# Second unit's attention values computed from high and low parts, and the low part of g moved to GpSimd in the first MLP, in a fused attention and MLP kernel

## The chip, the cores and the metric

The kernel runs on one core of one Trainium2 chip. The time is that of one execution on the device, in microseconds (us). A core has a matrix engine (TensorE, called PE in the profile, with its weight loads shown apart as PEld), a vector engine (DVE), an activation engine (ACT), a general engine (GpSimd, called POOL), and a queue that issues DMAs (SyncE, called SP). Each engine takes its instructions in a fixed order. PE writes to PSUM; the other tiles named here lie in SBUF unless said otherwise.

## What is computed

Sliding-window attention with four sink keys for 4 batches of 8 heads (768 tokens, head size 64), then an MLP on the result (3072 tokens, 512 to 2048 to 512), all in float32:

```python
scores = scale * np.matmul(q, k.transpose(0, 1, 3, 2))
is_sink = pos[None, :] < int(n_sink)                  # n_sink = 4
in_window = (rel >= 0) & (rel < int(window))          # window = 128
scores = np.where(is_sink | in_window, scores, -1000000000.0)
a = np.exp(scores - np.max(scores, axis=-1, keepdims=True))
a = a / (np.sum(a, axis=-1, keepdims=True) + 1e-09)
x = np.matmul(a, v)        # then [batch*token, 512]
h = x @ w_in
g = np.maximum(0.01 * h, h)
return g @ w_out
```

## The kernel before

**Units.** The work is cut into 8 units of 384 tokens (T = 3 tiles of 128), two to a batch. Each unit has an attention part (8 heads, in 4 pairs) and an MLP part (16 blocks fc of 128 hidden columns). While PE computes the MLP of unit u, it computes the attention of unit u+1 in between; a generator for each gives the next few matmuls, and a due time in the last loop of `fast_path` weaves the two together. PE's order is exactly the order in which the code is written; the orders of DVE, ACT, POOL and SP come from a scheduler that puts instructions in the order of a simulated timeline. Unit 0's attention runs alone at the start (with warm-up matmuls in it); from 61 us on the MLP of unit 0 runs with the attention of unit 1.

**Exact products.** A float32 matmul on the tiles as they are ("native") is issued as two matmuls, each with its own weight load. The other way is to split a tile in a high part (the value rounded to the type fp32r) and a low part (the value minus the high part, rounded again) and to add products of parts, each one fp32r matmul. The MLP does that everywhere: `xh`, `xl` (line 507), `gh`, `gl` (lines 572, 573), and weights `wih`, `wil`, `woh`, `wol`.

**Attention.** For each head and tile j: `scores` (line 314), the softmax on DVE and ACT (lines 334 to 344; result in `pk`), then `tail`, which transposes `pk` on PE and copies it to `pt`. For each pair, `sinks` transposes the four sink columns, and DVE spreads them to `sn` (line 416). Then `values` (line 448) multiplies `pt` and the sinks by the values. In units 0 and 1 (`NATP = 8` pairs) this is done natively: `vn` is the loaded tile itself, 64 columns to a head, and both heads add into one PSUM bank, from which `emit_x` makes `xh` (ACT) and `xl` (DVE). From unit 2 on `split_values` (line 278) makes high and low parts of the loaded `vraw` and `vsraw` side by side in `vsp` and `ssp` (ACT and POOL), `tail` makes a low part of `pt` on DVE, the sinks get one too (`st`, line 423), and a head is 6 or 8 fp32r matmuls with 128 columns of weights and one for the sinks. The two 64-row halves of the result are then added (ACT line 458, DVE line 459) to `xf`.

**Weights.** `w_in` and `w_out` come as 64-bit words. `load_weights` (line 167) loads a 512 KB block into one of two buffers `wraw` (one block of `w_in`, then one of `w_out`, by turns), decodes it on DVE in three instructions (lines 176, 178, 180), and splits it on ACT (line 184) and POOL (line 185). The decode of block fc is issued when the MLP of unit 0 comes to block fc-2; blocks 0 to 2 are decoded in unit 0's attention, so 13 pairs of blocks (3 to 15) are decoded during unit 0's MLP. Both the MLP's g step and the weights' decode stand in DVE's one queue with the softmax.

**Loads of q, k and values.** SP's queue issues them with the weights' loads. A native head pair's values are loaded when the earlier pair has freed its tile (`vfree`), from inside the odd head before (line 489). The q and k of a head (`qkraw`) are split into `qksp` on ACT and POOL one head ahead, just after the first tile's softmax (`split_next`, line 494).

Of the kernel before, what the change touches and what calls it, by code (L numbers as in the profile page):

```python
# [9 lines left out]
F32 = mybir.dt.float32  # L10
F32R = mybir.dt.float32r
# [3 lines left out]
ALU = mybir.AluOpType  # L15
# [13 lines left out]
NU = 2 * B  # L29
NATP = 8  # L30
NATP0 = 0
# [14 lines left out]
LEAD0 = 5  # L46
GLP = 0
NACT = 6
# [73 lines left out]
def fast_path(ctx, tc, cpool, wz, qk, vu, vs, w_in, w_out, out, ident, lim, masks, tri, diag,  # L122
# [154 lines left out]

    def split_values(u, h):
        vr, sr = vraws.pop((u, h))
        vsp = apool.tile([P, 4, 2 * P], F32R, tag="vsp", name=f"vsp{u}_{h}", bufs=1)  # L280
        ssp = phase["late"].tile([SKR, 1, 2 * P], F32R, tag="ssp", name=f"ssp{u}_{h}", bufs=1)
        for dst, src, m in ((vsp, vr, NVB[u % 2]), (ssp, sr, 1)):
            sview = src[:, 0:m * P].rearrange("p (n q c) -> p n q c", q=2, c=D)
            hview = dst.rearrange("p n (q c) -> p n q c", c=D)[:, 0:m, 0::3, :]
            nc.scalar.copy(out=hview, in_=sview)
            nc.gpsimd.tensor_tensor(out=dst[:, 0:m, D:3 * D].rearrange("p n (q c) -> p n q c", c=D),
                                    in0=sview, in1=hview.bitcast(F32), op=ALU.subtract)
        return vsp, ssp
# [74 lines left out]
    def tail_wide(u, h, j, pk, pt, sk):  # L363
        half = u % 2
        tp = slot()
        n = 0
        o = 2 * P * j if half else max(0, (2 * j - 1) * P)
        for at in ((0, WM) if j or half else (0,)):
            nc.tensor.transpose(out=tp[:, n:n + P], in_=pk[:, j, at:at + P], identity=ident)  # L369
            n += P  # L370
        keep_warm(u, WARMT)
        nc.scalar.copy(out=pt[:, 0, o:o + n], in_=tp[:, 0:n])
        if j == T - 1:
            nj = T - 1 + half
            nc.scalar.copy(out=sk[:, 0:nj, h % 2], in_=pk[:, T - nj:, P:WM])
# [30 lines left out]

    def sinks(u, pair, sk):
        half = u % 2
# [10 lines left out]
        if native_values(u, 2 * pair):  # L419
            return sv  # L420
        st = sts[half]
        nc.scalar.copy(out=st[0:rows, :], in_=sv)
# [4 lines left out]
    def values(u, h, pt, st, state):  # L427
# [3 lines left out]
        hp = slice(odd * D, (odd + 1) * D)  # L431
        lp = slice((1 - odd) * D, (2 - odd) * D)
        vv, sv = state["v"]
        if native_values(u, h):
# [29 lines left out]
    def attend(u, h, pend, state):  # L464
# [8 lines left out]
        if not odd:  # L473
            state = state[h // 2 % 2]
            state["v"] = vraws.pop((u, h)) if native_values(u, h) else split_values(u, h)
            state["sk"] = apool.tile([P, T, 2, NSK], F32, tag="sk", name=f"sk{u}_{h // 2}")
        else:
            state = state[h // 2 % 2]
# [8 lines left out]
        for j in range(T):  # L487
            nxt = following(u, h)
            if j and odd and nxt and native_values(*nxt) and nxt not in vraws and (vfree[nxt[1] // 2 % 2] or j > 1):
                load_values(*nxt)  # L490
            ps = scores(u, h, j, parts, rows, sp)
            softmax(u, h, j, ps, pk[:, j, 0:KSL[u % 2][j][1]] if u < WIDE else pk[:, j, :])
            if u < WIDE and j == 0:
                split_next(u, h)
            yield
            at = len(pend) - (VSW and j == 0 and not odd and len(pend) > 0)
            pend.insert(at, lambda j=j: tail(u, h, j, pk, pt, sk))
        if odd:
            def gather():
                state["st"] = sinks(u, h // 2, sk)  # L500
                if u == 0 and h < H - 1:
                    load_weights(h // 2)
# [17 lines left out]
    def attention_stream():  # L520
# [5 lines left out]
        pump()  # L526
        load_values(0, 2)
        for u in range(NU):
# [298 lines left out]
```

## Time and profile before

| | us |
|---|---|
| three runs | 745.74, 746.28 (median), 749.74 |
| the profiled execution | 745.78, with a span of 743.8 in the trace and 1.98 around it |
| PE busy, of the span | 719.4 (97%) |
| DVE busy | 562.5 (76%) |
| ACT busy | 434.0 (58%) |
| POOL busy | 381.4 (51%) |

The span is the time from the first to the last instruction that the trace holds. PE's share of 97% is an average: in the first 61 us, where the attention of unit 0 runs alone, and from there to 158 us, PE has gaps; from there to the last tiles it has almost none. A stretch must be read by itself: how busy each engine is in it, and on which engine a wait ends last. DVE instructions overlap a little at their ends, so that the busy time of a stretch is less than the sum of the durations in it.

### The profile page before, as it was taken

The page shows a single profiled execution, that of the slowest core. Times are in us where ns is not written, and L with a number is a line of the kernel's source. Part 1 is how long each engine was busy: PE and PEld are TensorE (multiplying, and loading weights), DVE is VectorE, ACT ScalarE, POOL GpSimd, SP SyncE. Part 2 cuts the span into 40 slices and gives each one's busy share as a digit, 9 for nine tenths or more (in the row PEclk, how much of TensorE's full clock was granted, in tenths as well). Part 3 has the DMA queues.
Part 4 walks back from the last instruction along what each step waited for, and adds up shares of the span by engine and source line. Part 5 has one row for each costly group of instructions (what it writes and reads, how often), then busy time and mean ns, then how long its engine had stood idle before and what let it go on. Part 6 is the DMA issues. An engine that isn't in the chain of part 4 may idle for free.

```text
span 743.8 us, 12686 instructions
## 1 busy us (share of the span) xinstructions
PE 719.4 (97%) x3935; PEld 624.2 (84%) x3935; DVE 562.5 (76%) x1832; ACT 434.0 (58%) x1208; POOL 381.4 (51%) x490
## 2 busy tenths in 40 slices
PE   8889999989999999999999999999999999999996
PEld 4557777768999988999988988989889899989995
DVE  6866889877667888888888888889888978733222
ACT  4666667657665666666566666666666656532221
POOL 3554455455445677665666587665666555300000
PEclk9979999999999999999999999999999999999999
DMA  5543666543212343224333443334331321001001
GB/s 181 181 146 117 186 196 195 187 146 100 59 51 68 115 125 119 89 93 156 115 108 102 126 137 99 105 96 146 116 110 52 111 69 44 1 1 42 1 1 46
DMA packets 30474, 76.94 MB, mean 103 GB/s; under 512 B 3584, under 2 KB 9152, under 8 KB 30400
## 3 DMA queue, kind: packets, MB, share of 16 engines
q1 hardware_dynamic: 30256, 75.94, 32.7%
q8 instruction: 33, 0.54, 0.3%
q14 instruction: 41, 0.34, 0.1%
q10 hardware_dynamic: 144, 0.13, 0.1%
HBM read 69.76 MB, written 6.29 MB: 102 GB/s over the span
## 4 chain that ended last, share of the span: by engine, by line
PE 84%; DVE 9%; ACT 3%; issue 1%; DMA 1%; POOL 0%; SPq 0%; ACTq 0%; DVEq 0%
PE o L584 32%; PE h L563 32%; PE v L448 9%; PE s L314 5%; PE t L382 2%; PE warm L304 2%; DVE gl L573 2%; PE t L369 1%; DVE zeroi L197 1%; DVE pk L344 1%; ACT qksp L271 1%; DVE g L571 1%; DMA woraw<-in_w_out 1%; DMA qkraw<-in_qk 0%; DVE pk L334 0%
## 5 line engine op out<-in xcount | busy, mean ns | idle before, releaser
L563 PE MATMUL h<-xh,wih 128*128 128x384 f32 x512 | 187.8, 367 | 1.5 <-DVE g L571 1.3
L563 PE MATMUL h<-xh,wil 128*128 128x384 f32 x512 | 173.0, 338 | 1.5 <-POOL wil L185 1.5
L563 PE MATMUL h<-xl,wih 128*128 128x384 f32 x512 | 172.5, 337 | 0.0
L584 PE MATMUL o<-woh,gh 128*128 128x512 f32 x384 | 154.3, 402 | 0.0
L584 PE MATMUL o<-woh,gl 128*128 128x512 f32 x384 | 151.2, 394 | 0.0
L584 PE MATMUL o<-wol,gh 128*128 128x512 f32 x384 | 151.1, 393 | 0.0
L353 POOL TENSOR_SCALAR_AFFINE_SELECT pt<-stg 128x256 fp32r<-128x256 f32 x240 | 101.4, 448 | 83.3 <-DVE stg L395 70.9
L272 POOL TENSOR_TENSOR qksp<-qkraw,qksp 64x524 fp32r<-64x524 f32 (+1 forms) x62 | 75.0, 1209 | 107.2 <-issue 62.7
L573 DVE TENSOR_TENSOR gl<-g,gh 128x384 fp32r<-128x384 f32 x128 | 105.8, 826 | 17.1 <-ACT gh L572 15.6
L571 DVE TENSOR_TENSOR g<-h,g 128x384 f32<-128x384 f32 x128 | 71.1, 555 | 60.2 <-ACT g L570 58.1
L563 PEld LDWEIGHTS h<-xh,wih 128*128 128x128 f32 x512 | 96.6, 189 | 16.1 <-issue 2.9
L570 ACT ACTIVATE g<-h 128x384 f32<-128x384 f32 x128 | 62.2, 486 | 69.7 <-PE h L563 68.4
L338 ACT ACTIVATE pk<-pk,negm 128x128 f32<-128x128 f32 (+2 forms) x168 | 70.2, 418 | 54.0 <-DVE negm L334 53.0
L563 PEld LDWEIGHTS h<-xl,wih 128*128 128x128 f32 x512 | 97.0, 189 | 3.0
L563 PEld LDWEIGHTS h<-xh,wil 128*128 128x128 f32 x512 | 96.2, 188 | 1.8 <-POOL wil L185 1.8
L314 PEld LDWEIGHTS s<-qksp 128*128 128x128 f32 x372 | 68.8, 192 | 21.9 <-issue 10.4
L584 PEld LDWEIGHTS o<-woh,gl 128*128 128x128 f32 x384 | 72.1, 188 | 16.3 <-DVE gl L573 0.2
L572 ACT CAST gh<-g 128x384 fp32r<-128x384 f32 x128 | 65.7, 513 | 33.6 <-DVE g L571 31.3
L314 PE MATMUL s<-qksp 128*128 128x260 f32 (+1 forms) x372 | 77.0, 289 | 8.6 <-DVE pk L344 5.2
L584 PEld LDWEIGHTS o<-woh,gh 128*128 128x128 f32 x384 | 72.5, 189 | 11.2 <-issue 2.4
L584 PEld LDWEIGHTS o<-wol,gh 128*128 128x128 f32 x384 | 72.4, 188 | 6.4
L274 POOL TENSOR_TENSOR qksp<-qkraw,qksp 128x384 fp32r<-128x384 f32 x62 | 67.9, 1095 | 4.7
(124 smaller groups left out, 1222.8 us busy)
## 6 DMA issues: line engine op xcount, KB each, us to landing
qkraw<-in_qk SPq DMA_DIRECT2D x32, 454.0 KB, 4.1
qkraw<-in_qk SPq DMA_DIRECT2D x30, 388.0 KB, 3.3
wiraw<-in_w_in SPq DMA_DIRECT2D x16, 512.0 KB, 3.6
woraw<-in_w_out SPq DMA_DIRECT2D x16, 512.0 KB, 4.0
ciraw<-in_w_in SPq DMA_DIRECT2D x16, 512.0 KB, 3.6
coraw<-in_w_out SPq DMA_DIRECT2D x16, 512.0 KB, 3.8
out<-ob SPq DMA_DIRECT2D x23, 256.0 KB, 2.0
vraw<-in_vu SPq DMA_DIRECT2D x12, 256.0 KB, 2.6
```

The costliest lines, as they stand in the source:

```text
L272: nc.gpsimd.tensor_tensor(out=sp[D:P, TU:TU + n], in0=raw[D:P, TU:TU + n], in1=sp[D:P, TU:TU + n].bitcast(F32), op=ALU.subtract)
L274: nc.gpsimd.tensor_tensor(out=sp[:, TU + n:2 * TU + n], in0=raw[:, 0:TU], in1=sp[:, 0:TU].bitcast(F32), op=ALU.subtract)
L314: nc.tensor.matmul(ps[:, 0:kn], lhsT=sp[rows, off + j * P:off + (j + 1) * P], rhs=sp[rows, TU + k0:TU + k0 + kn], start=c == 0, stop=c == ...
L338: nc.scalar.activation(out=e, in_=e, func=AF.Exp, scale=-1.0, bias=neg, accum_out=sm)
L353: nc.gpsimd.affine_select(out=out, in_=src, pattern=([[0, x]] if x > 1 else []) + [[sign, P]], base=-1 if prev else 0, channel_multiplier= ...
L448: nc.tensor.matmul(out[:, o:o + m], lhsT=l, rhs=r, start=c == 0, stop=c == len(mms) - 1, skip_group_check=True)
L563: nc.tensor.matmul(ph[:, 0:TU], lhsT=w[:, cs], rhs=x, start=cc == 0 and c == 0, stop=cc == NCC - 1 and c == 2)
L570: nc.scalar.mul(g, ph[:, 0:TU], 0.01)
L571: anchor[0] = nc.vector.tensor_tensor(out=g, in0=ph[:, 0:TU], in1=g, op=ALU.max)
L572: nc.scalar.copy(out=gh, in_=g)
L573: (nc.gpsimd if u == 0 and fc % 4 < GLP else nc.vector).tensor_tensor(out=gl, in0=g, in1=gh.bitcast(F32), op=ALU.subtract)
L584: nc.tensor.matmul(po[t], lhsT=gg[:, tsl], rhs=w, start=f == 0 and c == 0, stop=f == NFC - 1 and c == 2)
```

## The change

Native values stay for unit 0 only (`NATP = 4`). Unit 1's values go the way of the later units: high and low parts of the values (ACT, POOL), a low part of `pt` on DVE, and the sum of two halves to `xf`. As the tiles of the later units (`ssp`, `st0`, `st1`) don't exist yet in unit 1, a tile `it` in the place of a buffer that is free after unit 0 takes the sinks (first 384 columns, zeroed by a DVE memset and an ACT copy) and the sinks' values (last 256). Since unit 1 isn't native any more, `emit_x` makes its `xl` on POOL instead of DVE. `GLP = 4` moves the low part `gl` in all 16 blocks of unit 0's MLP from DVE to POOL. Native values (unit 0) are loaded at tile 1 of their own even head. The split of q and k for heads of unit 1 and later in the first two units is issued one tile later.

```diff
-NATP = 8
+NATP = 4
...
-GLP = 0
+GLP = 4
...
+    def interim(u, h):
+        it = phase["early"].tile([SKR, TU + 2 * P], F32R, tag="qkraw2", name=f"it{u}_{h}", bufs=1)
+        zeros = xpool.tile([P, TU], F32, tag="xf", name=f"zeros{u}_{h}")
+        nc.vector.memset(zeros, 0.0)
+        nc.scalar.copy(out=it[:, 0:TU], in_=zeros)
+        return it
+
-    def split_values(u, h):
+    def split_values(u, h, it):
         vr, sr = vraws.pop((u, h))
         vsp = apool.tile([P, 4, 2 * P], F32R, tag="vsp", name=f"vsp{u}_{h}", bufs=1)
-        ssp = phase["late"].tile([SKR, 1, 2 * P], F32R, tag="ssp", name=f"ssp{u}_{h}", bufs=1)
+        if u < WIDE:
+            ssp = it[:, TU:].rearrange("p (o c) -> p o c", o=1)
+        else:
+            ssp = phase["late"].tile([SKR, 1, 2 * P], F32R, tag="ssp", name=f"ssp{u}_{h}", bufs=1)
...
         nc.scalar.copy(out=pt[:, 0, o:o + n], in_=tp[:, 0:n])
+        if not native_values(u, h):
+            nc.vector.tensor_tensor(out=pt[:, 1, o:o + n], in0=tp[:, 0:n], in1=pt[:, 0, o:o + n].bitcast(F32),
+                                    op=ALU.subtract)
...
-        st = sts[half]
+        st = it[:, 0:TU] if u < WIDE else sts[half]
...
+        if native_values(u, h) and not odd:
+            state["v"] = vraws.pop((u, h))
...
-            state["v"] = vraws.pop((u, h)) if native_values(u, h) else split_values(u, h)
+            if not native_values(u, h):
+                state["it"] = interim(u, h) if u < WIDE else None
+                state["v"] = split_values(u, h, state["it"])
...
         for j in range(T):
-            nxt = following(u, h)
-            if j and odd and nxt and native_values(*nxt) and nxt not in vraws and (vfree[nxt[1] // 2 % 2] or j > 1):
-                load_values(*nxt)
+            if j == 1 and not odd and native_values(u, h) and (u, h) not in vraws:
+                load_values(u, h)
             ps = scores(u, h, j, parts, rows, sp)
...
-            if u < WIDE and j == 0:
+            nxt = following(u, h)
+            if u < WIDE and j == min(nxt[0], 1):
                 split_next(u, h)
...
         load_values(0, 0)
         pump()
-        load_values(0, 2)
```

Three places show how the order moves. First, PE, unit 1, head 4 (`v1_4`; `o0_0` is an output tile of unit 0's MLP). Before:

```order
L448 MATMUL v1_4_1642<-pt1_4_1204,vn1_4_1123 64x128
L448 MATMUL v1_4_1642<-pt1_4_1204,vn1_4_1123 64x256 x2
L448 MATMUL v1_4_1642<-pt1_4_1204,vn1_4_1123 64x128
L448 MATMUL v1_4_1642<-sn1_2_1615,vsn1_4_1124 64x384
L584 MATMUL o0_0_888<-woh9_1346,gh0_9_1554 128x512
L584 MATMUL o0_0_888<-wol9_1347,gh0_9_1554 128x512
```

and after the change:

```order
L463 MATMUL v1_4_1732<-pt1_4_1257,vsp1_4_1250 128x128 x2
L463 MATMUL v1_4_1732<-pt1_4_1257,vsp1_4_1250 128x256 x4
L463 MATMUL v1_4_1732<-pt1_4_1257,vsp1_4_1250 128x128 x2
L463 MATMUL v1_4_1732<-it1_4_1246 128x384
L600 MATMUL o0_0_901<-woh9_1404,gh0_9_1634 128x512
L600 MATMUL o0_0_901<-wol9_1405,gh0_9_1634 128x512
```

Five native matmuls (each issued as two) become nine in fp32r; all that stands around a head on PE stays where it was.

Second, DVE, at the end of unit 1 (`wid15` and `wod15` are the decode of the last weights, `pk2_0` with `s2_0_0` and `s2_0_1` the first softmaxes of unit 2, `tri` a mask). Before:

```order
L176 TENSOR_SCALAR wod14_1778<-woraw14_1766 128x512
L178 SCALAR_TENSOR_TENSOR wod14_1778<-woraw14_1766,wod14_1778 128x512
L511 TENSOR_TENSOR xl1_3_1897<-v1_6_1879,xh1_3_1896 128x384
L180 SCALAR_TENSOR_TENSOR wo14_1777<-woraw14_1766,wod14_1778 128x512
L334 ISA pk2_0_1924,negm_65<-s2_0_0_1926,m0_86 128x128
L334 ISA negm_65 128x1
L176 TENSOR_SCALAR wid15_1838<-wiraw15_1833 128x512
L323 COPY_PREDICATED s2_0_1_1937<-tri_88,s2_0_1_1937 128x128
```

and after the change:

```order
L180 SCALAR_TENSOR_TENSOR wi15_1947<-wiraw15_1943,wid15_1948 128x512
L176 TENSOR_SCALAR wod15_1957<-woraw15_1945 128x512
L178 SCALAR_TENSOR_TENSOR wod15_1957<-woraw15_1945,wod15_1957 128x512
L474 TENSOR_TENSOR xf1_3_2001<-v1_7_2010,xf1_3_2001 64x384
L180 SCALAR_TENSOR_TENSOR wo15_1956<-woraw15_1945,wod15_1957 128x512
L344 ISA pk2_0_2050,negm_65<-s2_0_0_2052,m0_86 128x128
L344 ISA negm_65 128x1
L145 MEMSET zeros_2037 128x384
L148 CAST st0_2039<-zeros_2037 128x256
L148 CAST st1_2041<-zeros_2037 128x384
L333 COPY_PREDICATED s2_0_1_2063<-tri_88,s2_0_1_2063 128x128
```

The whole decode of weights 15 now stands ahead of unit 2's first softmax, where before it stood among the first four.

Third, SP, around the load of the q and k of unit 1's head 1 (`qkraw1_1`). Before:

```order
L159 DMA woraw2_533<-in_w_out 128x1024
L239 DMA vn1_0_682<-in_vu1 128x512
L223 DMA qkraw1_1_654<-in_qk1 128x908
L159 DMA wiraw3_678<-in_w_in 128x1024
L240 DMA vsn1_0_683<-in_vs 24x128
L159 DMA woraw3_680<-in_w_out 128x1024
```

and after the change:

```order
L159 DMA woraw2_533<-in_w_out 128x1024
L223 DMA qkraw1_1_672<-in_qk1 128x908
L244 DMA vraw1_0_639<-in_vu1 128x512
L246 DMA vsraw1_0_641<-in_vs 128x128
L159 DMA wiraw3_682<-in_w_in 128x1024
L159 DMA woraw3_684<-in_w_out 128x1024
```

The load of q and k no longer stands behind the load of the values, which waits for a tile that unit 0's third pair frees.

## Rows read from the trace of the kernel before

**Rows 1.** Busy time of each engine in four stretches (start and end, length, then busy us and instructions of PE, PEld, DVE, ACT and POOL, the granted PE clock, the share of the DMA engines, GB/s).

```profile
65.10:159.50 94.40, 89.63 (x464) 70.10 (x465) 80.97 (x206) 64.22 (x164) 51.04 (x43) 1.00 0.59 185
88.00:132.00 44.00, 42.54 (x224) 33.67 (x223) 40.33 (x102) 32.02 (x82) 25.07 (x21) 1.00 0.61 191
135.00:145.00 10.00, 9.37 (x55) 8.09 (x53) 9.66 (x25) 8.12 (x22) 6.84 (x7) 1.00 0.63 201
158.20:656.00 497.80, 496.06 (x2821) 448.43 (x2822) 412.08 (x1394) 311.76 (x890) 303.00 (x415) 1.00 0.31 96
```

**Rows 2.** The chain of waits from 149 to 159 us (start, length, what).

```profile
149.32 2.24 PE v L448 x10
151.59 0.49 ACT xh L510
...
152.57 0.64 DVE wo L180
...
153.28 3.75 DMA woraw<-in_w_out
...
158.22 0.41 PE s L314 x2
```

**Rows 3.** PE in order of time around a native head of unit 1 (start, length, engine, line, operation, tiles, shape; the rows of several matmuls are merged).

```profile
124.72 0.34 PE L563 MATMUL h<-xh,wil 128*128 128x384 f32 x1
124.99 1.51 PE L448 MATMUL v<-pt,vn 128*64 128x128 f32 x8
...
127.56 0.40 PE L584 MATMUL o<-wol,gh 128*128 128x512 f32 x1
```

**Rows 4.** The same around a split head of unit 3, which has the same four key blocks.

```profile
256.51 0.39 PE L584 MATMUL o<-woh,gl 128*128 128x512 f32 x1
256.74 1.02 PE L448 MATMUL v<-pt,vsp 128*128 128x128 f32 x8
...
258.05 0.39 PE L584 MATMUL o<-wol,gh 128*128 128x512 f32 x1
```

**Rows 5.** Transition from unit 0 to unit 1, in order of time: POOL's last read of `qkraw1_0`, SP's issue of `vn1_0` and of `qkraw1_1`, and ACT's split of the latter (in brackets the idle time before, and what ended it); then the first weight decode of the next stretch.

```profile
43.87 1.01 POOL L274 TENSOR_TENSOR qksp<-qkraw,qksp 128x384 fp32r<-128x384 f32 x1
...
45.75 0.33 SPq L239 DMA_DIRECT2D vn<-in_vu  x1
46.18 0.37 SPq L223 DMA_DIRECT2D qkraw<-in_qk  x1
...
49.91 0.95 ACT L271 CAST qksp<-qkraw 128x908 fp32r<-128x908 f32 x1 [1.41 <-DMA qkraw<-in_qk]
...
65.11 0.68 DVE L176 TENSOR_SCALAR wid<-wiraw 128x512 int32<-128x512 int32 x1
```

**Rows 6.** Groups of DVE instructions between 65.1 and 159.5 us (count, busy us, mean ns of one, idle us of DVE just before them, and what ended it).

```profile
L573 DVE TENSOR_TENSOR gl<-g,gh 128x384 fp32r<-128x384 f32 x14 | 9.8, 701 | 0.0
L176 DVE TENSOR_SCALAR wid<-wiraw 128x512 int32<-128x512 int32 x13 | 9.0, 693 | 2.6 <-DMA wiraw<-in_w_in 2.5
L176 DVE TENSOR_SCALAR wod<-woraw 128x512 int32<-128x512 int32 x13 | 9.0, 692 | 6.0 <-DMA woraw<-in_w_out 5.9
L571 DVE TENSOR_TENSOR g<-h,g 128x384 f32<-128x384 f32 x15 | 8.3, 551 | 0.6 <-ACT g L570 0.4
L511 DVE TENSOR_TENSOR xl<-v,xh 128x384 fp32r<-128x384 f32 x4 | 2.2, 552 | 2.9 <-ACT xh L510 2.9
```

**Rows 7.** The same for DVE between 180 and 280 us, in the later units: low parts of `pt` (here one block of 128 columns), the sum to `xf`, the low part of the sinks.

```profile
L395 DVE TENSOR_TENSOR stg<-t,stg 128x128 fp32r<-128x128 f32 x24 | 7.0, 290 | 2.3 <-ACT stg L393 2.0
L459 DVE TENSOR_TENSOR xf<-v,xf 64x384 f32<-64x384 f32 x9 | 4.9, 548 | 3.7 <-ACT xf L458 3.7
L423 DVE TENSOR_TENSOR st<-sn,st 24x384 fp32r<-24x384 f32 x2 | 1.1, 548 | 0.6 <-ACT st L422 0.6
```

**Rows 8.** DVE in order of time, single instructions: a wait for `xh`, the end of unit 1 with the start of unit 2, and the zeros for the later units.

```profile
109.40 0.56 DVE L511 TENSOR_TENSOR xl<-v,xh 128x384 fp32r<-128x384 f32 x1 [0.99 <-ACT xh L510]
...
152.57 0.68 DVE L180 SCALAR_TENSOR_TENSOR wo<-woraw,wod 128x512 int32<-128x512 int32 x1
153.17 0.29 DVE L334 CUSTOM_DVE_ANT_0 pk<-s,m 128x128 f32<-128x128 f32 x1
...
157.12 0.69 DVE L176 TENSOR_SCALAR wod<-woraw 128x512 int32<-128x512 int32 x1 [0.93 <-DMA woraw<-in_w_out]
...
162.05 0.38 DVE L145 MEMSET zeros<- 128x384 f32 x1
...
162.75 0.55 DVE L148 CAST st<-zeros 128x256 fp32r<-128x256 f32 x2
```

**Rows 9.** Groups of POOL instructions: the first between 65.1 and 159.5 us, the others between 180 and 280 us.

```profile
L274 POOL TENSOR_TENSOR qksp<-qkraw,qksp 128x384 fp32r<-128x384 f32 x8 | 8.1, 1014 | 0.6
...
L511 POOL TENSOR_TENSOR xl<-xf,xh 128x384 fp32r<-128x384 f32 x4 | 4.7, 1184 | 2.1 <-ACT xh L510 2.1
L286 POOL TENSOR_TENSOR vsp<-vraw,vsp 128x512 fp32r<-128x512 f32 x2 | 2.7, 1331 | 1.2 <-ACT vsp L285 1.2
```

**Rows 10.** Groups of ACT instructions between 180 and 280 us.

```profile
L458 ACT COPY xf<-v 64x384 f32<-64x384 f32 x9 | 4.3, 473 | 1.0 <-PE v L448 0.9
L285 ACT CAST vsp<-vraw 128x512 fp32r<-128x512 f32 x2 | 1.2, 607 | 0.0
L422 ACT CAST st<-sn 24x384 fp32r<-24x384 f32 x2 | 1.0, 512 | 1.5 <-DVE sn L416 1.5
```

More of the change, by code (lines that the diff above doesn't have):

```diff
@@ L405, in tail, with sinks @@
             (nc.gpsimd if SKP else nc.vector).tensor_copy(out=sk[:, 0:nj, h % 2], in_=pk[:, T - nj:, 0:NSK])
-    def sinks(u, pair, sk):
+    def sinks(u, pair, sk, it):
         half = u % 2
@@ L499, in gather @@
             def gather():
-                state["st"] = sinks(u, h // 2, sk)
+                state["st"] = sinks(u, h // 2, sk, state.get("it"))
                 if u == 0 and h < H - 1:
```

## Prediction, made before the changed kernel was run

> **What bounds the kernel now.** I read the busy times by stretch first. From 158.2 to 656 us PE is busy 496.1 of 497.8 us [rows 1]: nothing in that stretch is worth anything unless it takes work from PE, and the order there is the same in both kernels. So the change is decided before 158 us. The stretch from 65.1 to 159.5 us, from the decode of weights 3 to the end of that of weights 15, is another case: PE is busy 89.6 of 94.4 us, DVE 81.0 (86%), ACT 64.2, POOL 51.0 [rows 1]. PE leads, but DVE is close behind. The chain of waits shows how close: at the end of unit 1 it leaves PE. The last value matmuls end, ACT makes `xh`, DVE is held by `xl`, so the third step of the decode of `w_out` 14 starts only at 152.57; then the buffer is free, the next block is loaded in 3.75 us, and PE's softmax input waits until 158.22 [rows 2]. PE's clock is 1.00 in all of it [rows 1], so no clock level is at stake.
>
> **PE: what is removed.** Native, from the start of the matmul before a head to the second one behind it 127.56 - 124.72 = 2.84 us pass [rows 3]. In a split head of unit 3 it is 258.05 - 256.51 = 1.54 us [rows 4]. The neighbour in front is 0.06 us shorter in the native case (a matmul of 384 columns and not 512, about 0.17 and 0.23 us from start to start), so a head gains 1.36 us and the eight heads of unit 1 gain **10.9 us** of PE. In the stretch PE's work falls from 89.6 to 78.7 us, and DVE is then the fuller engine even with the work that it has now.
>
> **DVE: what is added and removed, up to the end of the decode of weights 15.** Instructions overlap by about 0.08 us (152.57 to 153.17 is 0.60 us for one of 0.68 [rows 8]), so each counts as its duration less 0.08.
> - Low parts of `pt`, 256 columns out of PSUM: the trace has 128 columns (0.290 us [rows 7]) and 384 (0.551, the g step [rows 6]). In the middle, 0.42; 23 of the 24 fall in the stretch: 23 x 0.34 = 7.8.
> - Sums to `xf`: 8 x (0.548 - 0.08) [rows 7] = 3.8. Low parts of the sinks: 4 x 0.47 [rows 7] = 1.9. Zeros for the later two pairs: 2 x 0.30 [rows 8] = 0.6.
> - Gone: 14 `gl` at 0.701 [rows 6], 8.7. Four `xl` at 0.552 [rows 6], 1.9. Six instructions of unit 2's first softmaxes, which stood ahead of the last decode and now stand behind it, about 0.21 each (the 0.29 of [rows 8]), 1.3.
>
> Added 14.1, gone 11.9: **DVE's work up to that point rises by 2.2 us, from 81.0 to 83.2.** The move of `gl` just pays for what the split values cost DVE.
>
> **POOL and ACT.** POOL gets 14 `gl` (as `qksp` of the same size, 1.014), 4 `xl` (1.184), three `vsp` (1.331) [rows 9] and the small sinks' values, under half of a `vsp` each: 51.0 + 14.2 + 4.7 + 4.0 + 2 = 76 us of 94. I cost this at nothing in itself: the readers of `gl` are the output matmuls of the block, which PE takes a block later, behind the next block's 12 h matmuls. The cover has a hole: `g` has one buffer, so ACT's next `g` waits for POOL's `gl`, and POOL has the splits of a pair in front of it in its queue, `vsp` and `xl` among them, 1.33 + 1.18 = 2.5 us; if DVE's g were late by all of that once a pair, it would cost 4 x 2.5 = 10 us, and if never, 0. I put it in the idle time below and not in a term of its own. ACT gets 8 copies to `xf` (0.473), four of values (0.607), four of sinks (0.512) [rows 10] and, at most the same each, four of zeros and four of sinks' values: at most 64.2 + 3.8 + 2.4 + 2.0 + 4 = 76 us. Both are below DVE.
>
> **The start of unit 1.** Now SP holds the load of `qkraw1_1` until 46.18, behind the load of `vn1_0`, although POOL's last read of its buffer ends at 44.88, and ACT then sits 1.41 us for it [rows 5]. Moved ahead, the load can start 1.2 us sooner. Against that stand ACT's new copies and, ahead of the first g, `xl` of unit 0's last pair behind one more softmax. Bounds 0 and 1.2; I take 0.6, so weights 3 start at 64.5 instead of 65.1 [rows 5].
>
> **The end of unit 1.** Unit 2's softmax now stands behind `wo15`, and PE cannot pass its second score tile before the first is read (one PSUM bank). From that first softmax (153.17 [rows 8]) to the fourth score tile on PE (158.22 [rows 2]) 5.05 us pass. Out of these go a DMA wait of 0.93 and four decode instructions of 0.60 each, 2.4; in come the zeros and their two casts, 0.30 + 0.47 [rows 8]: 2.5 us. From the fourth score tile on PE is full and the rest of the program has the same work.
>
> **The sum.** The gain is 158.2 - (64.5 + 83.2/s + 2.5), or 91.2 - 83.2/s, where s is DVE's share of busy time. The trace has three values for s. It was 0.858 over the stretch. It was 40.33/44 = 0.917 over its fullest 44 us, and 0.938 without the 1.0 us in it in which DVE waited for `xh` [rows 1, 8], a wait that goes to POOL. It was 0.966 over the fullest 10 us [rows 1]. I take the middle of 0.917 and 0.938, since the new waits for `xf` (3.7 us for nine in the later units [rows 7]) come in the place of those for `xh`: s = 0.928, 83.2/s = 89.7, gain **1.5 us**. The profiled run took 745.78, so 744.3; the median of the runs stands 0.5 above it, so **744.8**. The break-even is s = 0.912.
>
> **Rivals.**
> - *PE stays the bound.* Then all of the 10.9 and the 0.6 count: 734.8. For it speaks that PE has the largest share now. Against it: 91.2 - 10.9 = 80.3 us would be left for DVE's 83.2, so DVE would have to be more than full; only if the added instructions cost much less than their nearest rows can it come near.
> - *DVE runs fuller.* DVE no longer waits for PE, its weights are issued earlier in its queue, and the waits for `xh` are gone: s = 0.966 as in the fullest 10 us gives 86.1, a gain of 5.1, 741.2. For it: that stretch was reached with weights, softmax and g all in the queue. Against it: 8.4 of DVE's 13.4 idle us are waits for weights to land [rows 6], with two buffers and 3.75 us to load one [rows 2]; these do not go away with a faster PE.
> - *DVE waits as much as now* (the other side). Only the kind of wait changes: the loads' waits stay, and each of the eight `xf`, four sinks and 23 `pt` steps waits for an ACT copy, and g for POOL's `gl`, in one queue with the decode, so that every wait delays the next load too. s stays at 0.858, 83.2/s = 97.0, and the kernel is 5.8 us slower: 752.1. It decides below s = 0.912, and can be measured below 0.877. For it: the later units show 6.6 us of such waits in 100 us [rows 7], and there PE was the one that was late.
>
> In this stretch DVE was busy 86% and PE's weight loads 70.1 of 94.4 us, 74% [rows 1]. The Trainium skill, Perfetto Trace Analysis, section Identifying the Most-Contended Engine, says to compare VectorE by its occupancy and TensorE by its LDWEIGHTS share and not by its matmul share, and to work on the fullest engine; by that rule DVE was the bound already and taking work from PE is no help. The time by it would be that of the last rival; the trace agrees in that the chain leaves PE for DVE and a load at the end of the stretch, and speaks against it in that PE was busy 42.5 of the 44 us in which DVE was fullest.
>
> **How the numbers follow.** A difference under 0.5% (3.7 us) cannot be told from none in a measurement of this kernel. My forecast, a stretch set by DVE with s between 0.90 and 0.945 (743.1 to 747.5), has a chance of 0.52; through the bounds of the start of unit 1 and of the low parts' price, 0.03 of it lie beyond 0.5% faster and 0.02 beyond 0.5% slower. PE as the bound has 0.08, a fuller DVE 0.22, unchanged waits 0.18. Faster by over 0.5%: 0.08 + 0.22 + 0.03 = 0.33. Within: 0.47. Slower: 0.18 + 0.02 = 0.20. The range leaves out the first rival and the upper tail of the last: 740.5 to 751.0.
>
> **What would show it.** In the changed kernel's profile the head of unit 1 should take about 1.1 us on PE, and from 65 us to unit 2 PE should have gaps, 8 us or more, that end on DVE; there DVE should be busy 91 to 95%, with its waits still mostly on weights. Unit 2's fourth score tile should start near 156.7 us. If PE has hardly a gap there, the first rival is right; if DVE shows under 88% with waits on `xf`, `pt` or g, the third. The forecast is wrong from the ground if low parts of `pt` are far from 0.42 us, or if POOL, and not DVE, is what PE and ACT wait for.

## The result, and the profile after

The changed kernel takes 753.47 us (median of 7 runs, 751.45 to 756.32) against 746.49: a ratio of **1.0088, 95% interval 1.0070 to 1.0106**, slower by 6.6 us by this ratio. Ratios go by fast runs alone: one slow execution each of run 6 (1394.56 us) and run 15 (871.12 us) is left out of them. The forecast was 744.8, the range 740.5 to 751.0. The profiled run is the longest of the seven, 756.32 us with a span of 754.5.

Two stretches (columns as in [rows 1]): from the decode of weights 3 to the end of that of weights 15, and a stretch of the later units.

```profile
64.89:160.26 95.37, 82.27 (x436) 70.36 (x436) 82.93 (x211) 70.13 (x173) 70.74 (x64) 0.95 0.59 180
165.36:642.00 476.64, 475.40 (x2685) 429.25 (x2685) 392.36 (x1330) 300.83 (x861) 296.02 (x400) 1.00 0.32 99
```

The later units are full on PE as before. In the first stretch DVE has 82.93 us of work, almost to the tenth what the prediction counted (83.2), but needs 95.37 us for it: a share of 0.870. PE did get its relief. This is a head in order of time (as [rows 3]); from the matmul before it to the second one behind it 81.57 - 80.12 = 1.45 us pass, where it was 2.84:

```profile
80.12 0.34 PE L579 MATMUL h<-xh,wil 128*128 128x384 f32 x1
80.31 1.03 PE L463 MATMUL v<-pt,vsp 128*128 128x128 f32 x8
81.17 0.39 PE L463 MATMUL v<-it 128*128 128x384 f32 x1
81.40 0.34 PE L579 MATMUL h<-xh,wih 128*128 128x384 f32 x1
81.57 0.34 PE L579 MATMUL h<-xl,wih 128*128 128x384 f32 x1
```

The relief came back as waiting (`negm` is the softmax's negated row maximum, `sm` its row sum, `t` a transpose's PSUM tile, `s` a score tile). PE's waits up to unit 2's fourth score tile (who waits at which line, for whom; us in total, times, the longest) are 16.1 us from 61 us on, where they were 5.9 with the one right ahead of that tile:

```profile
PE t L379 <- DVE pt L384: 4.9, 5, 2.1
PE t L425 <- DVE pt L384: 2.8, 2, 2.4
PE h L579 <- DVE g L587: 2.3, 3, 1.0
PE s L324 <- DVE negm L344: 2.2, 2, 1.1
PE s L324 <- DVE sm L350: 1.7, 1, 1.7
PE t L425 <- DVE sm L349: 1.5, 1, 1.5
```

All are for DVE, and 7.7 us for the new low parts of `pt`. The 10.2 us more of waits eat the relief of 10.9. Beyond that, PE's own matmuls up to that tile take 88.18 us in this run, where 91.33 less the relief would be 80.4: the clock was at 0.50 in some 12 of these us (last section); in run 5, at 1.00, they take 83.81. The transposes of unit 1 have a single PSUM tile, since the decode uses the other (`slot()` gives `t0` alone in unit 0's MLP). Before, ACT's copy freed it; now DVE's low part does, in its turn in DVE's queue. One such wait, on PE and on DVE in order of time:

```profile
90.23 0.40 PE L324 MATMUL s<-qksp 128*128 128x260 f32 x2
92.78 0.44 PE L379 MATMUL t<-ident,pk 128*128 128x128 f32 x2 [2.15 <-DVE pt L384]
```

```profile
89.73 0.69 DVE L176 TENSOR_SCALAR wod<-woraw 128x512 int32<-128x512 int32 x1 [0.76 <-DMA woraw<-in_w_out]
90.46 0.56 DVE L474 TENSOR_TENSOR xf<-v,xf 64x384 f32<-64x384 f32 x1
91.05 0.69 DVE L178 SCALAR_TENSOR_TENSOR wod<-woraw,wod 128x512 int32<-128x512 int32 x1
91.78 0.56 DVE L587 TENSOR_TENSOR g<-h,g 128x384 f32<-128x384 f32 x1
92.25 0.14 DVE L349 TENSOR_SCALAR sm<-sm 128x1 f32<-128x1 f32 x1
92.31 0.41 DVE L384 TENSOR_TENSOR pt<-t,pt 128x256 fp32r<-128x256 f32 x1
```

DVE stands for a weight block that has not landed, then works through decode, `xf` and g; only then comes the 0.41 us that PE has wanted since 90.6. DVE's groups between 61 and 160 us (as [rows 6]) show that its own waits are still those for weights, 9.0 us:

```profile
L384 DVE TENSOR_TENSOR pt<-t,pt 128x256 fp32r<-128x256 f32 x23 | 9.5, 413 | 0.3 <-ACT pt L382 0.3
L176 DVE TENSOR_SCALAR wod<-woraw 128x512 int32<-128x512 int32 x13 | 9.0, 692 | 4.4 <-DMA woraw<-in_w_out 4.3
...
L176 DVE TENSOR_SCALAR wid<-wiraw 128x512 int32<-128x512 int32 x13 | 8.9, 687 | 4.7 <-DMA wiraw<-in_w_in 4.7
...
L474 DVE TENSOR_TENSOR xf<-v,xf 64x384 f32<-64x384 f32 x8 | 4.4, 550 | 0.8 <-ACT xf L473 0.7
```

The chain of waits has moved with them: over the stretch, weight loads are 41% of it (before, 4%, and PE's matmuls 83%; first line before, second after). A share of the chain isn't a price: in run 3 loads are 19% of it, at a time that can't be told from the kernel before.

```profile
by line: PE o L584 27.1%; PE h L563 27.1%; PE v L448 19.4%; PE t L369 5.0%; PE s L314 4.4%; DMA woraw<-in_w_out 4.1%; issue 3.7%; POOL qksp L272 1.5%; POOL wil L185 1.3%; POOL qksp L274 1.1%; ACT qksp L271 0.8%; DVE wod L176 0.8%; DVE wo L1
by line: DMA woraw<-in_w_out 30.7%; DMA wiraw<-in_w_in 10.0%; DVE wod L176 6.5%; issue 6.0%; DVE wod L178 5.9%; DVE wo L180 5.8%; PE h L579 4.1%; DVE wi L180 3.4%; PE o L600 3.2%; DVE wid L176 2.7%; DVE xf L474 2.6%; DVE pk L344 2.5%; DVE g
```

### The profile page after: what moved, and what is told of

Its sections match the earlier page's. It is cut to its first block, busy times and chain, and to the rows that moved or that the text cites. A ratio compares the mean times of both kernels' runs of the same rounds, so it can differ in the third digit from the quotient of the medians.

```text
span 754.5 us, 12763 instructions
## 1 busy us (share of the span) xinstructions
PE 719.5 (95%) x3927; PEld 629.7 (83%) x3927; DVE 567.0 (75%) x1852; ACT 445.1 (59%) x1232; POOL 407.2 (54%) x518
## 4 chain that ended last, share of the span: by engine, by line
PE 75%; DVE 14%; DMA 6%; ACT 3%; issue 2%; POOL 0%; DVEq 0%; ACTq 0%; POOLq 0%
PE o L600 29%; PE h L579 29%; PE v L463 7%; PE s L324 5%; DMA woraw<-in_w_out 4%; PE t L395 2%; PE warm L314 2%; DVE gl L589 2%; DMA wiraw<-in_w_in 1%; DVE wod L178 1%; DVE zeroi L197 1%; DVE wod L176 1%; DVE pk L344 1%; DVE pk L354 1%; DVE wo L180 1%
## 5 line engine op out<-in xcount | busy, mean ns | idle before, releaser
L600 PE MATMUL o<-woh,gl 128*128 128x512 f32 x384 | 153.0, 398 | 0.0
L600 PE MATMUL o<-wol,gh 128*128 128x512 f32 x384 | 152.9, 398 | 0.0
L579 PEld LDWEIGHTS h<-xh,wih 128*128 128x128 f32 x512 | 97.2, 190 | 15.2 <-DVE g L587 4.0
L589 DVE TENSOR_TENSOR gl<-g,gh 128x384 fp32r<-128x384 f32 x112 | 92.2, 824 | 16.7 <-ACT gh L588 15.2
```

The lines of the kernel that those rows point to most:

```text
L579: nc.tensor.matmul(ph[:, 0:TU], lhsT=w[:, cs], rhs=x, start=cc == 0 and c == 0, stop=cc == NCC - 1 and c == 2)
L589: (nc.gpsimd if u == 0 and fc % 4 < GLP else nc.vector).tensor_tensor(out=gl, in0=g, in1=gh.bitcast(F32), op=ALU.subtract)
L600: nc.tensor.matmul(po[t], lhsT=gg[:, tsl], rhs=w, start=f == 0 and c == 0, stop=f == NFC - 1 and c == 2)
```

## The experiments

Theory A at first: DVE's queue is the bound, and the low part of `pt` frees PE's bank late. Rivals: B, gl on POOL costs; L, the weight loop does (a block is loaded, decoded by three steps in DVE's queue, and only then is its buffer loaded again). Each time is a median with the ratio to the kernel before on the same chip.

**1. gl back on DVE** (`GLP = 0`).

> The changed kernel with gl of unit 0 back on DVE; the split values of unit 1 and the moved loads stay. Theory A (DVE's queue sets the stretch: its low part of pt frees the one PSUM tile of the transposes late, and every instruction more on DVE makes it later): DVE's work in the stretch rises from 82.9 by 14 x 0.62 = 8.7 us, and at the share of 0.87 that the changed kernel shows this is 10 us: about 763. Rival B (gl on POOL, through the single buffer of g, is what costs): faster than the changed kernel, 750 or less.

755.1 us, 1.0104 (1.0066 to 1.0142): not to be told from the changed kernel. Fourteen gl more on DVE raised its share, from the decode of weights 3 to the end of that of weights 15, to 91.89 of 98.55 us, 0.932, without a price that shows. The move also takes them off POOL, so it doesn't price DVE's work alone.

```profile
66.76:165.31 98.55, 82.08 (x449) 69.82 (x449) 91.89 (x234) 72.19 (x180) 59.26 (x51) 0.98 0.59 177
```

B falls, and so does A in the form "DVE's work is the bound".

**2. Native values, the rest of the change kept** (`NATP = 8`).

> The changed kernel with the native fp32 values of unit 1 back; gl stays on POOL and the loads stay moved. Theory A: DVE falls to about 72 us, PE is the bound with 89.6 us of work, and at most its 3.8 us of waits for DVE can go: 743 to 746, with the clock of the kernel before, 0.988. Rival B (gl on POOL): the waits of ACT's g and of the output matmuls for POOL show up here too, 749 or more.

747.9 us, 1.0011 (0.9997 to 1.0026), between the two cases. Against run 3, which differs from it in gl alone, gl on POOL neither gains nor costs.

**3. The moved loads and splits alone** (`NATP = 8`, `GLP = 0`).

> Only the moved loads and splits: native values in unit 1, gl on DVE. From the prediction's term for the start of unit 1: 745.3 to 746.5. If the move itself is what costs (a value load behind weights 0, a split a tile later), 748 or more.

748.0 us, 1.0011 (0.9996 to 1.0026). No gain. Runs 1 to 3 leave the split values as the loss.

**4. Two PSUM banks for the transposes.**

> The changed kernel, with the decode's intermediate in the SBUF tile of its result and not in a PSUM bank, so that the transposes of unit 1 alternate between two PSUM banks. Theory A, in the form that the one bank is the cause: the 7.7 us in which PE waits for the low part of pt go nearly all, fewer falls of the clock behind them: 744 to 748. Rival C (DVE is simply full, with its waits for weights, so PE is held by it at the next place): the waits move to g, negm and the sums, and the time stays at 751 to 754.

```
-            wi = pool.tile([P, 512], I32, tag=tag, name=f"w{nm}d{fc}")
+            wi = w.bitcast(I32)
...
-        tag = f"t{slots[0] % 2}" if phase.get("mlp", 1) else "t0"
+        tag = f"t{slots[0] % 2}"
```

771.5 us, 1.0327 (1.0309 to 1.0344). PE's waits for `pt` fell to 0.8 us, but the decode, now from and to SBUF, became much dearer, and PE waited for g (8.2 us), negm (6.8) and the sinks (6.7). Two of its groups, which were 0.69 and 0.68 us:

```profile
L180 DVE SCALAR_TENSOR_TENSOR wi<-wiraw,wi 128x512 int32<-128x512 int32 x13 | 14.7, 1133 | 0.1
L182 DVE SCALAR_TENSOR_TENSOR wi<-wiraw,wi 128x512 int32<-128x512 int32 x12 | 13.4, 1115 | 0.0
```

The test is spoilt by its side effect and decides nothing on A.

**5. One bank in two halves.**

> The changed kernel, with the one PSUM bank of the transposes of unit 1 used in two halves in turn, so that PE may be a tile ahead of DVE's low part of pt; nothing else changes and no instruction is added. Theory A (the single tile is the cause): the 7.7 us of PE's waits for the low part go, 745 to 748. Theory L (the loop of a weight block sets the pace: load of 4.5 us, three decode steps on DVE with other work between them, and the next load only then): PE waits at the next place that hangs on DVE instead, 751 to 754.

```
+        if not phase.get("mlp", 1):
+            at = slots[0] % 2 * 2 * P
+            return phase["bank"][:, at:at + 2 * P]
```

752.9 us, 1.0075 (1.0052 to 1.0098). PE still waited 9.0 us for `pt`, in the two longest waits for the tile just before, so the halves were not free of each other: no test of A either.

**6 and 7. Weights loaded by half,** in the changed kernel and in the one before.

> The changed kernel with the weights of blocks 4 to 15 loaded by half (256 of 512 columns, used twice, so the other half of these weights is left out of the MLP); DVE's decode has the same number of elements. Theory L: the load falls from 4.5 to about 2.4 us, DVE's 9 us of waits for weights and most of PE's waits go, and PE's 10.9 us less of work can show: 736 to 744. Theory A (single tile): the low part of pt stands behind the same decode steps, 749 to 753.

> The same half loads in the kernel before, as the control. Theory L and theory A alike: PE is the bound there and waits for the weights only at the end of unit 1 and in the 1.5 us for wil: 743 to 746.

```
+            nc.sync.dma_start(out=raw.rearrange("p f t -> p (f t)")[:, 0:512], in_=src[:, 0:512])
...
+                top, low = (raw[:, 0:256, i].rearrange("p (o f) -> p o f", o=1).broadcast_to([P, 2, 256]) for i in (1, 0))
```

749.1 us, 1.0019 (1.0004 to 1.0034), and 745.0, 0.9977 (0.9959 to 0.9995). The loads shortened less than expected (about 3 us and not 2.4), yet gave the changed kernel 0.7% and the one before 0.2%. 749.1 lies at the low end of theory A's range and far above theory L's. The profile of run 6 says more: the stretch from the decode of weights 3 to the end of that of weights 15 is 7 us shorter than in the changed kernel, DVE's share of it is 82.94 of 88.44 us, 0.938, and it ends at 154.74; yet unit 2's fourth score tile starts only at 162.73, after 15.2 us of waits of PE. So the end of the decode doesn't set that tile.

```profile
66.30:154.74 88.44, 75.85 (x415) 64.83 (x416) 82.94 (x207) 67.35 (x168) 68.74 (x61) 0.98 0.40 123
162.73 0.41 PE L333 MATMUL s<-qksp 128*128 128x128 f32 x2 [0.30 <-DVE negm L353]
```

**8. Two of four pairs split** (`NATP = 6`).

> The changed kernel with split values in the last two pairs of unit 1 only (the first two native). If the cost is one of work, half of it: about 750. Theory L, in which PE can give up work only until the weight loop (some 7.3 us a block) is longer than PE's block: 743 to 747.

751.4 us, 1.0047 (1.0028 to 1.0066): half of the pairs, about half of the loss, as the case of work has it. No threshold shows between.

**9 to 11. ACT frees the bank,** the low part by DVE, by POOL, and by POOL with half of gl there too.

> The changed kernel, where ACT copies the transposed block of unit 1 a second time, unrounded, into columns of the softmax tile that are no longer used, and DVE takes the low part of pt from there: PE's bank is free after two ACT copies and no longer after DVE. ACT gets 24 x 0.37 = 9 us more (70 to 79 of 95), DVE has the same instructions, perhaps dearer ones from SBUF. Theory A (the bank that DVE frees late): PE's 7.7 us of waits for the low part go, 745 to 749. Theory L (weight loads and their decode on DVE): PE waits for g, negm or the sums instead, 751 to 755.

> As the run in which ACT frees the bank, but with the low part of pt on POOL and gl of unit 0 back on DVE: POOL 70.7 - 14.1 + 24 x about 0.7 = 73 us, DVE 82.9 - 9.5 + 9.6 = 83 us, so the work per engine is as in the changed kernel and only who frees and who makes the low part differs. Theory A: 745 to 749. Theory L: 751 to 755.

> As the run before, with half of gl on POOL: DVE 78 us, POOL 80 us of some 95, no engine over 85% but PE. Theory A: 743 to 747, at or below the kernel before. Theory L: a decode that DVE gets to sooner, 748 to 752.

```
+            raw = pk[:, j, :].rearrange("p (o c) -> p o c", c=WM)[:, :, 0:P]
+            nc.scalar.copy(out=raw, in_=tp[:, 0:n].rearrange("p (o c) -> p o c", c=P))
...
+            nc.gpsimd.tensor_tensor(out=lo, in0=raw, in1=hi.bitcast(F32), op=ALU.subtract)
```

On DVE: 756.5 us, 1.0145 (1.0101 to 1.0190); a low part out of SBUF took 764 ns and not 413 (why: last section). On POOL: 750.8, 1.0061 (1.0036 to 1.0085), and 750.6, 1.0047 (1.0025 to 1.0068). No wait for the low part is left in PE's list of the second, but it is as long as before:

```profile
PE v L465 <- DVE it L438: 4.0, 3, 1.6
PE s L324 <- DVE negm L344: 3.9, 3, 1.8
PE h L581 <- POOL wil L185: 2.3, 2, 1.8
PE t L379 <- ACT pk L385: 2.2, 5, 0.8
```

So ACT's freeing of the bank, with 24 copies more on ACT and the low part on POOL, brought 2 to 3 us in all, the 2 of run 10 not clear of the noise. What the late bank costs by itself these runs don't show. A falls as the whole cause: PE waits at the next place.

**12. ACT frees the bank, and half loads.**

> The run in which ACT frees the bank and DVE makes the low part, with the weights of blocks 4 to 15 loaded by half (the other half of these weights is left out of the MLP). If the freed bank and the weight loads are the two causes together, both go: 740 to 745. If the time stays at 748 or more, a third one, the many short hops through DVE's queue (g, negm, sm), holds PE.

754.0 us, 1.0089 (1.0057 to 1.0122), with DVE busy 92.6 of the 96 us from 64 to 160, since the low part from SBUF now took 877 ns. It says only that the two don't add up while DVE gets the dearer instruction.

**13. A third of the decode left out.**

> The changed kernel without the second of the three decode steps for the weights of blocks 4 to 15 (24 x 0.69 = 16.5 us less on DVE; the signs of these weights are left out). If DVE's load and its queue set the stretch: PE's waits fall from 16 to 5 us or less, 740 to 743. If the latency under PE's fixed order sets it, whatever DVE's load: 749 or more.

```
+            if fc <= PRE:
+                nc.vector.scalar_tensor_tensor(out=wi, in0=top, scalar=-0x40000000, in1=wi,
+                                               op0=ALU.bitwise_and, op1=ALU.bitwise_or)
```

747.6 us, 1.0007 (0.9987 to 1.0027). 16.5 us less on DVE gave 6.0 us, between the two cases. PE's waits stayed at 16.3 us with DVE busy 77%, as the second case has it: a busy DVE is not the condition for PE to wait. A part of the 6.0 is PE's clock, which was 1.00 up to the fourth score tile here and 0.94 in the changed kernel's profile. That tile starts at 159.39, 9.8 us behind the end of the decode (149.55).

**14. One more step between softmax and transposes** (`LAG = 3`).

> The changed kernel with one more step between a tile's softmax and its transposes on PE (LAG 3 and not 2). If the latency from scores to transposes is what PE waits for: 745 to 749. If DVE's load sets it: 752 to 755, the waits moved.

777.7 us, 1.0396 (1.0362 to 1.0431). From unit 2's fourth score tile on it needs 606.7 us and not 585.6, so the constant also slows the later units, and PE's waits in the stretch stay (17.8 us). No help.

**15. Without the low parts of pt.**

> The changed kernel without the low parts of pt in unit 1 (its matmuls read the high part twice, so the low part is left out of the result): PE has the same matmuls, DVE 9.5 us less, and ACT frees the bank. If the low part is the main cost of the change: 741 to 745, faster than before. If the rest (sums, sinks, the zeros, the shorter PE itself) costs as much: 747 to 751.

```
-            mms = [(vv[:, kb, cs], pt[:, c, po:po + m], qo, m)
+            mms = [(vv[:, kb, cs], pt[:, c if u >= WIDE else 0, po:po + m], qo, m)
```

748.6 us, 1.0010 (0.9993 to 1.0027): the low parts cost 0.8%, 6 us, and the rest still eats the whole relief, as the second case has it. Part of the 6 us is the clock here too: its executions have a mean clock of 0.983 to 0.994, those of the changed kernel 0.977 to 0.986.

**16. The kernel before, with PE relieved and nothing added.**

> The kernel before with two of the five native matmuls of each head of unit 1 left out (those of the second key block and of the sinks, 640 of 1152 columns, so these are left out of the result): about 1.24 us a head or 9.9 us less on PE, and nothing more on any engine. If PE was the bound with room behind it: 737 to 739. By my forecast's sum with DVE at 81.0 us of work and s = 0.928: 742.1. If the next bound stands right behind PE (s near 0.87): 745 to 747, and relieving PE was worth next to nothing from the start.

```
-            mms.append((sv[0:st.shape[0], hp], st, q0, TU - q0))
+            if u == 0:
+                mms.append((sv[0:st.shape[0], hp], st, q0, TU - q0))
+            else:
+                del mms[1]
```

743.9 us, 0.9960 (0.9943 to 0.9976). Some 9.9 us less on PE gave 3.0 (1.8 to 4.3): faster than the third case has it, slower than the sum's 742.1. In the profile the fourth score tile comes 4.9 us sooner than in the kernel before; what stands behind it then takes 588.0 us and not 585.6, for which no cause was traced. The chain over the same stretch points at what stopped the rest: 41% of it is weight loads at once, in a kernel that has no split value at all.

```profile
153.33 0.41 PE L314 MATMUL s<-qksp 128*128 128x128 f32 x2 [0.30 <-DVE negm L334]
```

```profile
by line: DMA woraw<-in_w_out 23.8%; DMA wiraw<-in_w_in 16.8%; issue 10.6%; DVE wo L180 5.9%; DVE wod L178 5.1%; DVE wod L176 4.6%; DVE wid L176 3.1%; ACT qksp L271 3.1%; DVE wid L178 2.8%; PE h L566 2.7%; DVE wi L180 2.5%; DVE g L574 2.5%; 
```

**17. The same with half loads.**

> The kernel before with two of five native matmuls of each head of unit 1 left out, and the weights of blocks 4 to 15 loaded by half (second key block, sinks and half of these weights are left out of the result). If the weight loop stands right behind PE: the further gain is clearly more than the 2 us that half loads give with all matmuls, 738 to 740.5. If it is not the loads but DVE's work: 742 to 744.

740.6 us, 0.9917 (0.9896 to 0.9939): half loads give 0.4% here and 0.2% with all of PE's work, at the edge of the first case, but the two gains are not apart by more than the noise. The chain returns to PE:

```profile
by line: PE h L575 23.4%; PE o L596 21.5%; PE v L460 8.3%; POOL wil L194 4.4%; PE s L323 4.2%; issue 4.2%; DMA woraw<-in_w_out 4.0%; PE t L378 3.1%; DVE wod L187 2.9%; POOL qksp L281 2.8%; POOL qksp L283 2.8%; ACT qksp L280 2.1%; DVE wo L18
```

**18. The changed kernel with half loads and less decode.**

> The changed kernel with half loads and without the second decode step for blocks 4 to 15 (half of these weights and their signs are left out). If DVE's waits for weights and DVE's load, each enough by itself, make PE wait: PE's waits fall to 8 us or less, 738 to 742. If the new hops (ACT copy, DVE low part, one PSUM bank) hold PE by their own latency: PE's waits stay at 12 us or more, 745 to 748.

742.8 us, 0.9947 (0.9931 to 0.9964), PE's waits 11.2 us: between the two cases. Against the changed kernel the gains are 0.7% for the loads, 0.8% for the decode, 1.4% for both. They add up; neither hides the other, and 5.6 us of waits for low parts remain even so.

No version with the whole result beats the kernel before; runs 2 and 3 come nearest, at 1.0011.

## Why the prediction was wrong, point by point

- **PE: what is removed.** Right: 1.33 us a head (with the 0.06 for the neighbour) against 1.36, and a head of 81.40 - 80.31 = 1.09 us.
- **DVE: what is added and removed.** Right: 82.9 against 83.2 us, the low part at 0.413 against 0.42.
- **POOL and ACT.** Some 5 us too high (70.7 us on POOL for 76, 70.1 on ACT for at most 76), without harm, and right in costing gl on POOL at nothing, as far as runs 1 to 3 tell.
- **The start of unit 1.** 64.89 and not 64.5: 0.2 us of gain, inside the bounds, and nothing by run 3.
- **The sum, and in it s, is the step that failed.** I took 0.928; it was 0.870, worth 95.4 - 89.7 = 5.7 us, of which perhaps 2 are the clock (run 5, at 1.00 throughout: 82.61 of 93.15 us, 0.887). At 0.928 DVE would have had 6.5 us of idle time in the stretch; it had 12.4, and 9.0 of them for weights, where it was 8.4 before. But s is not only mis-sized. The sum takes DVE's work divided by s for the time, lets unit 2 follow 2.5 us behind, and counts PE's gaps as room that costs nothing. Run 1 has s = 0.932, as high as I took it, and is no faster; run 6 has 0.938, and PE reaches the fourth score tile 8.0 us behind the end of the decode. What made PE late is what the sum put at nothing: PE, in its fixed order, stood 16.1 us for single results of DVE. So a us of DVE's work has no one price, as 1/s would have it: run 1 puts 9.8 us of gl on DVE at no price that shows, run 13 pays 6.0 us for 16.5, run 15 about 6 for 9.5. Why the fullest 44 us were so full (that loads had time to land there because PE was late) was argued and not shown.
- **The clock.** "No clock level is at stake" failed too: it read the clock of a PE without long waits. With the new waits it fell to 0.50 three times in the profiled run; for the median of the seven runs this is worth about 1 us (last section).
- **The end of unit 1** was mis-sized: from the first softmax of unit 2 to its fourth score tile it took 165.36 - 160.19 = 5.2 us and not 2.5. The two casts behind the zeros alone took 2.15 us (I had 0.47), and PE waited 1.12 and 1.65 us. They stood beside two instructions of POOL, and each ended about 0.2 us behind one of these; in the kernel before and in run 3, with POOL idle, the two took 0.55.

```profile
160.19 0.28 DVE L344 CUSTOM_DVE_ANT_0 pk<-s,m 128x128 f32<-128x128 f32 x1
...
160.93 2.15 DVE L148 CAST st<-zeros 128x256 fp32r<-128x256 f32 x2
160.56 1.02 POOL L528 TENSOR_TENSOR xl<-xf,xh 128x384 fp32r<-128x384 f32 x1
161.53 1.33 POOL L185 TENSOR_TENSOR wol<-wo,woh 128x512 fp32r<-128x512 f32 x1
165.36 0.66 PE L324 MATMUL s<-qksp 128*128 128x128 f32 x2
```

- From there to the end the profiled run needs 589.1 us and not 585.6. The terms are then 0.4 + 5.7 + 2.7 + 3.5 = 12.3 on the predicted span of 742.3 (744.3 less the 2.0 around the span), which is the 754.5 of the span to 0.1. About 2.4 of the 3.5 are a clock at 0.50 from 165.4 to 170.1 (below), by an estimate that takes half of that time as lost; 1.0 lies behind the last matmul, from whose start to the end 8.0 us pass and not 7.0.
- **The rivals.** The one on the other side had about the right time (752.1; s of 0.858) and half of the mechanism. The time is in part luck: its stretch, 97.0 us, is longer than the 95.4 measured, and the end of unit 1 and the rest, which it took as in the forecast, were 6.2 us longer. The waits for the loads did stay (9.0 us). But DVE's waits for `xf`, `pt` and g are 1.7 us; the new waits are PE's, for DVE. That the low part frees the only PSUM tile of the transposes stood in none of the cases.

In its place the runs show three layers. Relieving PE by 9.9 us is worth 3.0 (run 16). By the chain it is the weight loop that stands right behind PE: the chain goes to the loads when PE is relieved and back when they are shortened (run 17); the times alone, 0.4% and 0.2% for half loads, don't show it. The low parts of `pt` cost 1.0088 - 1.0010, 5.8 us (run 15), with the late bank and a part of the clock's falls in it. What is left between run 16 and run 15, 0.5% or 3.7 us, belongs to the sums, sinks, zeros and the moved places together; how they share it was not tried. -3.0 + 3.7 + 5.8 is the loss of some 6.6 us; as the 3.7 is a difference of the other runs, that is no check. Why PE still waits 11.2 us with less decode and shorter loads (run 18) stays open: whether the copy by ACT, the step on DVE and the single tile do it by their own latency was argued and not isolated.

The prediction set its sum against a rule of the Trainium skill, Perfetto Trace Analysis, section Identifying the Most-Contended Engine, by which DVE was the fullest engine already. Run 16 agrees with neither: taking 9.9 us from PE gave 3.0 us, where the rule as read there has no gain and the sum at s = 0.928 has 742.1, some 4 us. And run 1 differs from what it would suggest: the fullest engine took more work at no price that shows.

## What to carry to other kernels

Where three engines and a load loop are all near full, price a us of work by who waits for it next, not by the fullest engine's share: here a us taken from PE paid 0.3, and a us on DVE cost between nothing that shows (gl, taken off POOL) and 0.6 (low parts of `pt`, with the late bank). Before adding a reader to a PSUM tile, look how many such tiles there are and what stands ahead of the reader in its queue. To know what relief is worth, leave the work out and add nothing: run 16 would have shown, before the change was written, that some 3 us were to be had, which the added work must not exceed.

## What the runs showed of the hardware

PE's clock, 1.00 from 61 to 656 us in the kernel before, fell three times to 0.50 (1.2 GHz) in the changed kernel's profiled run, twice 1 to 2.5 us behind a wait of PE and once within one. The windows, and two of the waits ahead:

```profile
105.30:108.60 3.30, 3.30 (x11) 2.82 (x11) 2.81 (x8) 2.22 (x5) 2.27 (x3) 0.50 0.34 132
...
142.90:149.50 6.60, 6.14 (x19) 4.87 (x19) 6.19 (x16) 4.47 (x13) 5.51 (x5) 0.50 0.67 205
149.70:160.50 10.80, 8.82 (x51) 7.31 (x49) 9.28 (x18) 5.88 (x13) 7.15 (x7) 1.00 0.51 153
163.40:170.00 6.60, 6.23 (x18) 4.95 (x19) 2.73 (x17) 4.44 (x14) 2.99 (x3) 0.50 0.26 80
```

```profile
104.09 0.28 PE L425 MATMUL t<-ident,sk 128*24 128x128 f32 x1 [2.36 <-DVE pt L384]
```

```profile
140.50 0.51 PE L324 MATMUL s<-qksp 128*128 128x260 f32 x2 [1.04 <-DVE negm L344]
```

The wait of 2.15 us at 92.78 brought no fall, and run 5, with 18.1 us of waits up to the fourth score tile, has 1.00 up to there and a median that is as long. What the falls cost is read from the changed kernel's own runs: the two with the highest mean clock, 0.986, which the kernel before has too (0.984 to 0.991 over its runs), took 751.81 and 752.70 us, and the two at 0.977 took 753.59 and 756.32. So the falls are worth some 4 us of this run's 756.3 and about 1 of the median, and at 0.986 the kernel is still over 5 us slower than 746.49.

DVE instructions with both inputs in SBUF were dearer in the mean than with one in PSUM: 764 ns against 413 for the same low part (877 in run 12), 1133 against 691 for a decode step. The single instructions show that this is not the price of SBUF but of POOL beside them. With POOL idle, the low part from SBUF took 0.40 or 0.41 us (two in run 9, three in run 12), as out of PSUM, and the decode step of run 4 0.66 to 0.69 us (eleven); beside a POOL instruction they took up to 1.57 and 1.67. The same decode step with an input in PSUM, in the changed kernel, took at most 0.70 beside POOL too. `gl` in the kernel before, 0.701 in the mean, is 0.54 to 0.56 with POOL idle and up to 1.60 beside it. Two low parts of run 9, the first with POOL idle, the second beside the POOL instruction below:

```profile
101.91 0.41 DVE L387 TENSOR_TENSOR pt<-pk,pt 128x256 fp32r<-128x256 f32 x1
81.46 1.40 DVE L387 TENSOR_TENSOR pt<-pk,pt 128x256 fp32r<-128x256 f32 x1
81.28 1.30 POOL L185 TENSOR_TENSOR wil<-wi,wih 128x512 fp32r<-128x512 f32 x1 [1.18 <-ACT wih L184]
```

The Trainium skill, SBUF — State Buffer, section SBUF: two separate sides, says that such an instruction shares a read port with GpSimd and that one of the two then waits out the other. The trace agrees: the second of these ended at 82.86, 0.28 us behind the end of the POOL instruction, and the means of run 9 were taken with POOL busy 73 of 96 us.
